# Attention and gated feed-forward on one core: the x of chunk 0 on GpSimd, earlier weight conversions, row sums turned with the last tile, the last rows in two halves

## The chip, the cores and the metric

The kernel runs on one core of a Trainium2 chip. A core has five engines that run side by side and wait for each other by semaphores: TensorE (PE, with its weight loads shown as PEld), VectorE (DVE), ScalarE (ACT), GpSimd (POOL), and SyncE (SP), which here only issues DMAs. The time is that of one execution on the device, in microseconds (us); the median of several runs counts. A span is the time from the first to the last instruction in a profile.

## What is computed

The reference, cut to what matters (4 batches, 8 heads, 576 positions, head dimension 64; then 2304 tokens, 512 columns, 1536 hidden columns):

```python
scores = scale * np.matmul(q, k.transpose(0, 1, 3, 2)) + bias      # bias: an MLP of relative positions, per head
attn = np.exp(scores - np.max(scores, axis=-1, keepdims=True))
attn = attn / (np.sum(attn, axis=-1, keepdims=True) + 1e-09)
x = np.matmul(attn, v)  # -> [2304, 512]
gate = 1.0 / (1.0 + np.exp(-(x @ w_gate)))
out = (gate * (x @ w_val)) @ w_out
```

All products are done to nearly fp32: an operand is split into a high part in a reduced format (`hi`, `aH`, `xhi`, `gh`) and the rest (`lo`, `aL`, `xlo`, `gl`), and hi·hi, hi·lo and lo·hi are summed.

## The kernel before

**Three stages.** First the bias of all heads is made and kept. Then attention runs over 16 units; unit u is a pair of heads p = u // 4 and a batch b = u % 4. Then the feed-forward part (class `Moe`) runs over 6 chunks of 384 tokens and 12 blocks f of 128 hidden columns.

**A unit of attention** has 9 steps s; n = 9u + s counts them all. A step issues, in an order that is written by hand: `score(n)` on TensorE into `sc`; `soft`, on DVE an operation that scales, adds the bias and takes the minimum (`en`, `mn`; L553), then on ACT the exponential with the row sum (L556); `turn(n - 2)`, which transposes an earlier `en` on TensorE into `pt` (L572, L592, and at step 8 L577), after which ACT writes `aH` and DVE writes `aL` (`split`, L471 and L472). For the steps in `AR` it is ACT that copies `pt` to `ar` and GpSimd that makes both parts (L465, L476). A few matmuls of `products` of the unit before fill each step (`FILL`); they sum in one PSUM buffer `acc`, so a new group of products can begin only when the copy `xe<-acc` (L635) on DVE has emptied it. `xe` goes to DRAM (`xs`).

**Row sums.** The nine columns of sums of a unit stand in the tile `sm`. `invert` adds 1e-9 on ACT (L611) and takes the reciprocal on DVE over 128 partitions and 9 columns (L612). `normal` transposes the result on TensorE (L598), DVE copies it to `rt` (9 partitions, 128 columns; L602), and two DMAs write it to `rs`.

**x of a chunk.** For each of the 4 head pairs kc, `load_x` and `load_r` fetch `xin` and `xrec` from `xs` and `rs`, and `prep_x` adds two halves (L797), multiplies by the reciprocal sums (L798), writes `xhi` on ACT (L799) and `xlo` (L800). For chunk 0 the table `PLAN` says at which step of the last four units (pair 3, steps counted from its first) each happens: l, r, x are loads and steps of chunk 0, capital letters those of chunk 1, s is one `stage`, the load of one more weight block. In chunk 0 only the add stands on GpSimd.

**Feed-forward.** For each (chunk, f) TensorE does 24 matmuls of `gates` into `pg` and `pu` (L864), then 9 of `outs` for the pair before (L885). In between, `gated` computes sigmoid on ACT, a product on DVE, and the split into `gh` and `gl` (L872 to L875). Chunks 0 (A) and 1 (B) are interleaved: A0 A1 B0 A2 B1 and so on. Weight blocks f = 0 and 1 are converted before; the others arrive as raw tiles `ww` and are made by `convert()`: on ACT L187, on DVE L190 to L199, on ACT `w<-wm` (L831), on DVE the lower part (L836). One call of `convert` begins one block and brings every begun block one stage on; a block is whole with its fifth call.

The instruction lists of all engines are in program order, and each engine runs its list in order.

Of the kernel before, what the change touches and what calls it, by code (L numbers as in the profile page):

```python
# [10 lines left out]
F32 = mybir.dt.float32  # L11
F32R = mybir.dt.float32r
# [3 lines left out]
AF = mybir.ActivationFunctionType  # L16
ALU = mybir.AluOpType

B, H, S, D = 4, 8, 576, 64
HID = 32  # L20
NT, DM, DFF = 2304, 512, 1536
NP = H // 2
# [3 lines left out]
FILL = (7, 0, 9, 0, 6, 3, 2, 7, 2)  # L26
ENB = 7
WM = 4
# [9 lines left out]
DPOS = [20, 36, 52], [6, 22, 38]  # L38
WARM = 12
CFI = 1  # L40
# [5 lines left out]
CONV = (2, 1)  # L46
START = 'X0 R1 X0 R2 X1 X2 X1 L3 s X2 X1 X1', 'R3 s X2 s s X3 X3 X2 X3 s X3'
XNEXT = {5: (("l", 0), ("r", 0)), 6: (("l", 1),), 7: (("p", 0), ("r", 1), ("l", 2)), 8: (("p", 1), ("r", 2), ("l", 3)),
# [3 lines left out]
PLAN = {  # L52
# [3 lines left out]
RAWS, WTS = 11, 18  # L56
SLOTS = (15, 18)
XENG = lambda nc, c: nc.vector if c else nc.gpsimd
AR = (1, 4, 7)
SOFT = (2, 7, 5, 3)  # L60
# [356 lines left out]
def attention(tc, att, q, k, v, biases, biasL, ident, xs, rs, extra):  # L417
# [3 lines left out]
    nc = tc.nc  # L421
# [3 lines left out]
    per = pool("per", 1)  # L425
# [4 lines left out]

    tiny = per.tile([128, 1], F32, name="tiny")
    nc.gpsimd.memset(tiny, 1e-9)
    QS = []
# [74 lines left out]
    vp = pool("vp", 1)  # L508
    enp = pool("enp", ENB)
    st = pool("st", 4)  # L510
    rtp = pool("rtp", 2)
    atp = pool("atp", 3)
    at4 = pool("at4", 2)
    ar_p = pool("arp", 2)
    xep = pool("xep", 2)
# [12 lines left out]
    def score(n):  # L528
        u, s = divmod(n, 9)
        p, b = units[u]  # L530
        ks, qs = prepped[u]
        if s == 0:
            state[u] = (st.tile([128, 9], F32, name="sm"), [], [], at4.tile([128, 2, S], F32R, name="a4"), {})
        ps = ps_s.tile([128, 2, 512], F32, name="sc")
        en = enp.tile([128, S], F32, name="en")
        sm = state[u][0][:, s:s + 1]
        state[u][4][s] = en
        if s < 8:
            h, it = divmod(s, 4)
# [12 lines left out]
        def soft():
            nc.vector.tensor_tensor_reduce(  # L553
                out=half(en), in0=ps[:, :, 0:HF], in1=half(nbias), scale=-0.125, scalar=3.0e38,
                op0=ALU.add, op1=ALU.min, accum_out=mn)
            nc.scalar.activation(out=en, in_=en, func=AF.Exp, bias=mn, scale=-1.0, accum_out=sm)  # L556

        return soft

    def turn(n):  # L560
# [12 lines left out]
        if s == 8:  # L573
            for h in range(2):
                after.append(split(aH[h][:, :, 512:576], aL[h][:, :, 512:576], pt[:, :, 64 * h:64 * h + 64]))
            pt = ps_t.tile([128, 4, 128], F32, name="pt")
            nc.tensor.transpose(pt[0:64, 0], en[:, 512:576], ident)  # L577
            last = normal(u, pt)
            after.append(split(a4[0:64, :, 512:576], a4[64:128, :, 512:576], pt[0:64, 0].rearrange("p (h i) -> p h i", h=2)))
            return after + [last]  # L580
        h, it = divmod(s, 4)
        i = slice(128 * it, 128 * it + 128)
        if s in AR:
            ar = ar_p.tile([128, 4, 128], F32, name="ar")
            nc.scalar.activation(out=ar, in_=pt, func=AF.Copy)
            pool_split(aH[h][:, :, i], aL[h][:, :, i], ar)
        else:
            after.append(split(aH[h][:, :, i], aL[h][:, :, i], pt))
# [6 lines left out]

    def normal(u, pt):
        p, b = units[u]
        nc.tensor.transpose(pt[0:9, 2], state[u][0], ident)  # L598
        rt = rtp.tile([9, 128], F32, name="rt")

        def leave():
            nc.vector.tensor_copy(out=rt, in_=pt[0:9, 2])  # L602
            to = rs[2 * p:2 * p + 2, S * b:S * b + S]
            nc.sync.dma_start(out=to[:, 0:512].rearrange("h (i p) -> h i p", p=128), in_=rt[0:8])
            nc.sync.dma_start(out=to[:, 512:576].rearrange("(o h) p -> o h p", o=1), in_=rt[8:9].rearrange("o (h p) -> o h p", h=2))

        return leave

    def invert(u):
        sm = state[u][0]  # L610
        nc.scalar.activation(out=sm, in_=sm, func=AF.Identity, bias=tiny)  # L611
        return lambda: nc.vector.reciprocal(out=sm, in_=sm)  # L612

# [29 lines left out]
    with tc.manual_schedule():  # L643
        work = iter(())
        after, due, loads, slow = [], [], [], []
        for n in range(9 * NU + LAG + 1):
            u, s = divmod(n, 9)
            soft = score(n) if n < 9 * NU else None
            inverse = invert(u - 1) if s == 0 and u > 0 else None
            later = turn(n - LAG) if LAG <= n < 9 * NU + LAG else []  # L650
# [21 lines left out]
            after = later  # L672
            if inverse:
                inverse()
            if s == WSTEP and 0 < u < NU:
# [22 lines left out]
class Moe:  # L698
# [53 lines left out]
    def do(self, what, eng=None):  # L752


        for w in what.split():
            i, c = int(w[1:] or 0), w[0] in "LRX"
            if w == "s":
                self.stage(eng)
            elif w == "t":
# [33 lines left out]
    def prep_x(self, c, t, r, hi, lo, kc):  # L793
        nc = self.nc
        x = t[:, 0]

        return [lambda: XENG(nc, c).tensor_tensor(out=x, in0=x, in1=t[:, 1], op=ALU.add),  # L797
                lambda: nc.vector.tensor_tensor(out=x, in0=x, in1=r, op=ALU.mult),  # L798
                lambda: nc.scalar.activation(out=hi[:, kc], in_=x, func=AF.Copy),  # L799
                lambda: nc.vector.tensor_tensor(out=lo[:, kc], in0=x, in1=hi[:, kc].bitcast(F32), op=ALU.subtract)]  # L800

# [85 lines left out]
    def store(self, c):  # L887
        for t, po in enumerate(self.po.pop(c)):
            if c == self.NC - 1 and t == 2:
                ob = self.pools["xin"].tile([128, 2, self.T], F32, name="xin").rearrange("p s t -> p (s t)")[:, 0:DM]  # L890
            else:
                ob = self.pools["ob"].tile([128, DM], F32, name="ob")
            self.nc.scalar.activation(out=ob, in_=po, func=AF.Copy)
            self.nc.sync.dma_start(out=self.out[self.T * c + 128 * t:self.T * c + 128 * t + 128, :], in_=ob)

    def run(self):
# [5 lines left out]
        with ExitStack() as ph, tc.manual_schedule():  # L902
# [6 lines left out]
            for i, cf in enumerate(order + [None]):  # L909
# [15 lines left out]
                for _ in range(CONV[c] - 1 if c < 2 else 0):  # L925
                    if self.going:
                        self.convert()
# [3 lines left out]
                if stored is not None:  # L931
                    self.store(stored)
                if self.going:
                    self.convert()
# [40 lines left out]
```

## Time and profile before

| | |
|---|---|
| median of 3 runs | 831.36 us (830.24 to 833.17) |
| profiled execution, its own time | 831.11 us |
| its span | 829.2 us |
| mean granted TensorE clock | 0.989 |
| TensorE matmuls busy | 797.5 us, 96% of the span |
| DVE, ACT, POOL busy | 61%, 52%, 31% |
| attention, about | 107 to 372 us |
| feed-forward, about | 362 to 826 us (its first gates stand among the last products of attention) |

In the page's slices TensorE is at nine tenths or more nearly throughout; the granted clock is full but for two places, near 317 to 323 us and near 388 to 395 us. The 1.9 us between span and time lie outside the instructions.

### The profile page before, as it was taken

What the parts mean: (1) busy time and instruction counts of PE and PEld (TensorE: products, weight loads), DVE (VectorE), ACT (ScalarE), POOL (GpSimd) and SP (SyncE); (2) the same over time, 40 slices, a digit from 0 to 9 for tenths busy, and PEclk for the clock granted to TensorE, in tenths of its full rate; (3) what the DMA queues carried; (4) which work ended last, traced back from release to release, by engine and by line L of the source; (5) the groups of instructions that cost most, each with busy time, mean ns of one, the idle gap of its engine ahead of it and who ended that gap; (6) DMA issues with size and microseconds to landing.
All of it is one profiled execution on the core that took longest, in us unless ns stands there. A gap on an engine that the chain in (4) does not pass through costs nothing.

```text
span 829.2 us, 16938 instructions
## 1 busy us (share of the span) xinstructions
PE 797.5 (96%) x6500; PEld 748.4 (90%) x6500; DVE 506.3 (61%) x1093; ACT 433.4 (52%) x918; POOL 261.2 (31%) x312
## 2 busy tenths in 40 slices
PE   7999989999999998977999999999999999999998
PEld 4888879999999998977999998999999999999997
DVE  6788879999998899966887884312411321241111
ACT  6888779899898996844444443211221221122112
POOL 1333669999998997730000000000000000000000
PEclk9999999999999998998999999999999999999999
DMA  5444336656556488749513301210030103011001
GB/s 192 130 146 146 97 75 171 164 134 185 148 158 170 140 241 230 216 155 355 192 52 104 99 1 52 89 51 28 10 115 1 40 30 85 0 39 39 1 1 38
DMA packets 51135, 89.56 MB, mean 108 GB/s; under 512 B 5616, under 2 KB 27248, under 8 KB 51056
## 3 DMA queue, kind: packets, MB, share of 16 engines
q1 hardware_dynamic: 48512, 85.28, 35.1%
q10 hardware_dynamic: 2544, 3.21, 1.2%
q8 instruction: 51, 0.84, 0.4%
q14 instruction: 28, 0.23, 0.1%
HBM read 61.66 MB, written 17.38 MB: 95 GB/s over the span
## 4 chain that ended last, share of the span: by engine, by line
PE 80%; DVE 12%; ACT 4%; issue 3%; DMA 0%; DVEq 0%; ACTq 0%
PE pg L864 18%; PE pu L864 18%; PE po L885 17%; PE acc L629 8%; PE sc L549 8%; PE pt L572 6%; PE bps L342 2%; DVE btmp L350 2%; ACT ind L323 1%; PE pt L592 1%; DVE bias L358 1%; DVE en L553 1%; PE y L318 1%; DVE xin L798 1%; ACT en L556 1%
## 5 line engine op out<-in xcount | busy, mean ns | idle before, releaser
L864 PE MATMUL pg<-xhi,w 128*128 128x384 f32 x576 | 161.1, 340 | 7.8 <-ACT w L831 2.8
L873 DVE TENSOR_TENSOR g<-pu,g 128x384 f32<-128x384 f32 x72 | 40.0, 556 | 209.6 <-PE pu L864 205.3
L864 PE MATMUL pu<-xhi,w 128*128 128x384 f32 x576 | 159.0, 336 | 0.0
L885 PE MATMUL po<-w,gh 128*128 128x512 f32 x432 | 133.8, 391 | 0.0
L556 ACT ACTIVATE en<-en,mn 128x576 f32<-128x576 f32 x144 | 111.5, 775 | 29.7 <-DVE mn L553 28.4
L864 PEld LDWEIGHTS pg<-xhi,w 128*128 128x128 f32 x576 | 105.9, 190 | 12.4 <-DVE w L836 3.3
L874 ACT ACTIVATE gh<-g 128x384 fp32r<-128x384 f32 x72 | 37.8, 525 | 147.9 <-DVE g L873 147.9
L549 PE MATMUL sc<-k,QS 128*128 128x288 f32 x640 | 112.8, 303 | 1.3 <-DVE bias L358 0.6
L864 PEld LDWEIGHTS pu<-xhi,w 128*128 128x128 f32 x576 | 105.2, 188 | 0.4 <-DVE w L836 0.4
L553 DVE CUSTOM_DVE_ANT_0 en<-sc,bias 128x576 f32<-128x576 f32 x128 | 94.0, 752 | 7.5 <-PE sc L549 6.5
L864 PE MATMUL pg<-xlo,w 128*128 128x384 f32 x288 | 97.5, 338 | 0.2 <-DVE xlo L800 0.2
L864 PE MATMUL pu<-xlo,w 128*128 128x384 f32 x288 | 96.7, 336 | 0.0
L549 PEld LDWEIGHTS sc<-k,QS 128*128 128x128 f32 x640 | 93.0, 191 | 2.4 <-PE sc L549 0.8
L872 ACT ACTIVATE g<-pg 128x384 f32<-128x384 f32 x72 | 35.1, 488 | 110.0 <-PE pg L864 108.9
L572 PE MATMUL pt<-ident,en 128*128 128x128 f32 x576 | 87.5, 275 | 3.6 <-DVE aL L472 2.6
L885 PEld LDWEIGHTS po<-w,gh 128*128 128x128 f32 x432 | 80.1, 188 | 12.0
L885 PE MATMUL po<-w,gl 128*128 128x512 f32 x216 | 84.2, 390 | 0.0
L629 PE MATMUL acc<-aH,vv 128*128 128x288 f32 x256 | 81.1, 334 | 3.0 <-DVE xe L635 1.9
L572 PEld LDWEIGHTS pt<-ident,en 128*128 128x128 f32 x576 | 69.1, 141 | 6.8 <-ACT en L556 3.1
L629 PE MATMUL acc<-aL,vv 128*128 128x288 f32 x256 | 71.6, 297 | 0.0
L472 DVE TENSOR_TENSOR aL<-pt,aH 128x512 fp32r<-128x512 f32 (+1 forms) x112 | 66.6, 607 | 7.1 <-ACT aH L471 7.1
L342 PE MATMUL bps<-cfs,ind 128*128 128x64 bf16 x1458 | 67.4, 193 | 3.2 <-DVE bias L358 2.5
(115 smaller groups left out, 1415.8 us busy)
## 6 DMA issues: line engine op xcount, KB each, us to landing
kr<-in_k_dram SPq DMA_DIRECT2D x32, 288.0 KB, 4.9
QS<-part SPq DMA_DIRECT2D x64, 144.0 KB, 2.6
xs<-xe SPq DMA_DIRECT2D x32, 288.0 KB, 3.9
xin<-xs SPq DMA_DIRECT2D x48, 192.0 KB, 3.5
vr<-in_v_dram SPq DMA_DIRECT2D x16, 320.0 KB, 3.7
qr<-in_q_dram SPq DMA_DIRECT2D x16, 288.0 KB, 3.6
xrec<-rs SPq DMA_DIRECT2D x48, 96.0 KB, 3.3
ww<-in_moe_w_out_dram SPq DMA_DIRECT2D x9, 512.0 KB, 6.9
```

The lines of the kernel that those rows point to most:

```text
L342: nc.tensor.matmul(out=o, lhsT=st, rhs=cfs[:, part], start=(part == 0), stop=(part == 2))
L472: return lambda: nc.vector.tensor_tensor(out=lo, in0=ps, in1=hi.bitcast(F32), op=ALU.subtract)
L549: nc.tensor.matmul(out=ps[:, e, 0:HF], lhsT=l, rhs=r[:, HF * e:HF * e + HF], start=(i == 0), stop=(i == len(mms) - 1))
L553: nc.vector.tensor_tensor_reduce(out=half(en), in0=ps[:, :, 0:HF], in1=half(nbias), scale=-0.125, scalar=3.0e38, op0=ALU.add, op1=ALU.min, ...
L556: nc.scalar.activation(out=en, in_=en, func=AF.Exp, bias=mn, scale=-1.0, accum_out=sm)
L572: nc.tensor.transpose(pt[:, J], en[:, 128 * J:128 * J + 128], ident)
L629: nc.tensor.matmul(out=acc[:, 0:HF], lhsT=l, rhs=r, start=(i == 0), stop=(i == len(mms) - 1))
L864: self.nc.tensor.matmul(out=(pg, pu)[z], lhsT=l, rhs=r, start=(kc == 0 and i == 0), stop=(kc == 3 and i == 2))
L872: nc.scalar.activation(out=g, in_=pg, func=AF.Sigmoid)
L873: nc.vector.tensor_tensor(out=g, in0=pu, in1=g, op=ALU.mult)
L874: nc.scalar.activation(out=gh, in_=g, func=AF.Copy)
L885: self.nc.tensor.matmul(out=po, lhsT=l[:, tt], rhs=r, start=(f == 0 and i == 0), stop=(f == self.NF - 1 and i == 2))
```

## The change

Nine things change together. (1) 16 instead of 12 warm-up matmuls. (2) The last tile of a unit (step 8) gets ten more columns, and the sums are written there (`en8`); the transpose of step 8 takes 73 columns instead of 64 and turns the sums with it. The transpose of `sm`, `invert` and `tiny` go. `normal` adds 1e-9 on DVE and takes the reciprocal there, over 9 partitions and 128 columns. (3) The tiles `en` get 6 buffers instead of 7, `ar` one instead of two. (4) In the last four units step 4 is split by ACT and DVE and no longer by GpSimd (`AR_LAST`). (5) The multiply and the subtract of x of chunk 0 move from DVE to GpSimd. (6) `PLAN` is rewritten. (7) Five loads of weight blocks, which stood among the steps of `START` and were issued by ACT, now stand first in it and are issued by SP. (8) `convert()` is also called when raw tiles wait though nothing has been begun, so it begins after the first gates and not at A2. (9) The last 128 rows leave as two halves: ACT copies and sends the left, DVE copies the right and SP sends it.

```diff
-ENB = 7
+ENB = 6
-WARM = 12
+WARM = 16
-START = 'X0 R1 X0 R2 X1 X2 X1 L3 s X2 X1 X1', 'R3 s X2 s s X3 X3 X2 X3 s X3'
+START = 's s s s s X0 R1 X0 R2 X1 X2 X1 L3 X2 X1 X1', 'R3 X2 X3 X3 X2 X3 X3'
 PLAN = {
-    2: "l0 l1", 3: "r0", 4: "s", 5: "r1", 6: "s", 8: "l2", 9: "x1", 10: "x0", 12: "x1 r2", 13: "x1 x0", 14: "x1 x0",
+    2: "l0 r0", 3: "l1 r1", 5: "s", 6: "x0 x0", 7: "x0 x0", 10: "l2 r2", 12: "s", 14: "x1 x1", 15: "x1", 16: "x1 s", 17: "L1",
...
-AR = (1, 4, 7)
+AR, AR_LAST = (1, 4, 7), (1, 7)
...
+    en8 = pool("en8", 2)
-    ar_p = pool("arp", 2)
+    ar_p = pool("arp", 1)
...
-            state[u] = (st.tile([128, 9], F32, name="sm"), [], [], at4.tile([128, 2, S], F32R, name="a4"), {})
+            last = en8.tile([128, S + 10], F32, name="en8")
+            state[u] = (last, [], [], at4.tile([128, 2, S], F32R, name="a4"), {8: last[:, 0:S]})
...
-            nc.tensor.transpose(pt[0:64, 0], en[:, 512:576], ident)
+            nc.tensor.transpose(pt[0:73, 0], sm[:, 512:S + 9], ident)
...
-        if s in AR:
+        if s in (AR if p < NP - 1 else AR_LAST):
...
-        nc.tensor.transpose(pt[0:9, 2], state[u][0], ident)
-            nc.vector.tensor_copy(out=rt, in_=pt[0:9, 2])
+            nc.vector.tensor_scalar(out=rt, in0=pt[64:73, 0], scalar1=1e-9, scalar2=None, op0=ALU.add)
+            nc.vector.reciprocal(out=rt, in_=rt)
...
-    def invert(u):
-        sm = state[u][0]
-        nc.scalar.activation(out=sm, in_=sm, func=AF.Identity, bias=tiny)
-        return lambda: nc.vector.reciprocal(out=sm, in_=sm)
...
-                self.stage(eng)
+                self.stage()
...
+        e = XENG(nc, c)
-        return [lambda: XENG(nc, c).tensor_tensor(out=x, in0=x, in1=t[:, 1], op=ALU.add),
-                lambda: nc.vector.tensor_tensor(out=x, in0=x, in1=r, op=ALU.mult),
+        return [lambda: e.tensor_tensor(out=x, in0=x, in1=t[:, 1], op=ALU.add),
+                lambda: e.tensor_tensor(out=x, in0=x, in1=r, op=ALU.mult),
                 lambda: nc.scalar.activation(out=hi[:, kc], in_=x, func=AF.Copy),
-                lambda: nc.vector.tensor_tensor(out=lo[:, kc], in0=x, in1=hi[:, kc].bitcast(F32), op=ALU.subtract)]
+                lambda: e.tensor_tensor(out=lo[:, kc], in0=x, in1=hi[:, kc].bitcast(F32), op=ALU.subtract)]
...
+            if c == self.NC - 1 and t == self.T // 128 - 1:
+                l, r = slice(0, DM // 2), slice(DM // 2, DM)
+                self.nc.scalar.activation(out=ob[:, l], in_=po[:, l], func=AF.Copy)
+                self.nc.scalar.dma_start(out=rows[:, l], in_=ob[:, l])
+                self.nc.vector.tensor_copy(out=ob[:, r], in_=po[:, r])
+                self.nc.sync.dma_start(out=rows[:, r], in_=ob[:, r])
...
-                    if self.going:
+                    if self.going or self.raw:
                         self.convert()
...
-                if self.going:
+                if self.going or self.raw:
                     self.convert()
```

The next lists are pieces of an engine's instructions in program order. First DVE in any unit from the second on, at its steps 1 to 3, before (`aL` and `a` are the lower parts of the last tile of the unit before, `bias_72` is the bias, the shape is that of the output):

```order
L472 TENSOR_TENSOR aL<-pt,aH 128x4x64 x2
L472 TENSOR_TENSOR a_4032<-pt,a_4032 64x2x64
L602 COPY rt<-pt 9x128
L553 ISA en,mn<-sc,bias_72 128x576
L553 ISA mn 128x1
L635 COPY xe<-acc 128x288
```

And the same place in the change, whose line numbers differ by a few (L554 is L553 of before, L632 is L635):

```order
L470 TENSOR_TENSOR aL<-pt,aH 128x4x64 x2
L470 TENSOR_TENSOR a_4027<-pt,a_4027 64x2x64
L603 TENSOR_SCALAR rt<-pt 9x128
L604 RECIPROCAL rt<-rt 9x128
L554 ISA en,mn<-sc,bias_72 128x576
L554 ISA mn 128x1
L632 COPY xe<-acc 128x288
```

A reciprocal of 128 columns now stands ahead of the softmax of step 3 and of the copy that empties `acc`.

Second, GpSimd in the first unit of the last pair, from its step 6 on, before (`k`, `vv` and `part` prepare k, v and q of the next unit):

```order
L465 TENSOR_SCALAR aH<-ar 128x4x128
L476 TENSOR_TENSOR aL<-ar,aH 128x4x128
L465 TENSOR_SCALAR vv_6379<-vr 128x5x64
L476 TENSOR_TENSOR vv_6379<-vr,vv_6379 128x5x64
L465 TENSOR_SCALAR k<-kr 128x576
L476 TENSOR_TENSOR k<-kr,k 128x576
L465 TENSOR_SCALAR aH<-ar 128x4x128
L476 TENSOR_TENSOR aL<-ar,aH 128x4x128
L797 TENSOR_TENSOR xin<-xin 128x384
```

And in the change:

```order
L792 TENSOR_TENSOR xin<-xin 128x384
L793 TENSOR_TENSOR xin<-xin,xrec 128x384
L463 TENSOR_SCALAR vv_6346<-vr 128x5x64
L474 TENSOR_TENSOR vv_6346<-vr,vv_6346 128x5x64
L795 TENSOR_TENSOR xlo<-xin,xhi 128x384
L463 TENSOR_SCALAR k<-kr 128x576
L474 TENSOR_TENSOR k<-kr,k 128x576
L463 TENSOR_SCALAR aH<-ar 128x4x128
L474 TENSOR_TENSOR aL<-ar,aH 128x4x128
```

The two operations on `ar` of step 4 have gone, and the add, the multiply and the subtract of x have come, around the preparation of v.

Third, ACT where attention ends and the feed-forward part begins, before (`xe` are the last products of attention, `g` the sigmoid of A0, `ww` raw weight blocks):

```order
L633 ACTIVATE xe<-acc 128x288 x3
L872 ACTIVATE g<-pg 128x384
L874 ACTIVATE gh<-g 128x384
L814 DMA ww<-in_moe_w_val_dram 128x4x256
L799 ACTIVATE xhi<-xin 128x384
```

And in the change:

```order
L630 ACTIVATE xe<-acc 128x288 x4
L794 ACTIVATE xhi<-xin 128x384
L187 ACTIVATE wm<-ww 128x512
L867 ACTIVATE g<-pg 128x384
L869 ACTIVATE gh<-g 128x384
L794 ACTIVATE xhi<-xin 128x384 x2
L187 ACTIVATE wm<-ww 128x512 x2
```

An `xhi` of chunk 1 and the first operation of the first conversion now stand ahead of the sigmoid of A0, and the DMA issues have left the engine.

## Rows read from the trace of the kernel before

**Rows 1.** The page: busy time, share of the span, instructions of each engine.

```profile
PE 797.5 (96%) x6500; PEld 748.4 (90%) x6500; DVE 506.3 (61%) x1093; ACT 433.4 (52%) x918; POOL 261.2 (31%) x312
```

**Rows 2.** Stretches: length; busy PE, PEld, DVE, ACT, POOL; granted clock, DMA share, GB/s.

```profile
200.00:250.00 50.00, 50.00 (x404) 49.72 (x403) 45.88 (x116) 45.67 (x111) 45.70 (x51) 1.00 0.61 167
...
300.00:340.00 40.00, 36.57 (x265) 35.35 (x264) 36.27 (x81) 31.30 (x75) 33.72 (x36) 0.91 0.87 237
340.00:360.00 20.00, 18.90 (x148) 17.83 (x147) 18.77 (x43) 16.81 (x41) 12.56 (x15) 1.00 0.55 169
...
372.00:400.00 28.00, 22.79 (x108) 20.75 (x108) 18.93 (x36) 12.43 (x23) 0.00 (x0) 0.88 1.02 342
```

**Rows 3.** Timeline of DVE in one unit: start, duration (us), line, operation.

```profile
182.61 0.21 DVE L612 RECIPROCAL sm<-sm 128x9 f32<-128x9 f32 x1
...
186.75 0.28 DVE L602 COPY rt<-pt 9x128 f32<-9x128 f32 x1
186.96 0.75 DVE L553 CUSTOM_DVE_ANT_0 en<-sc,bias 128x576 f32<-128x576 f32 x1
...
187.63 0.45 DVE L635 COPY xe<-acc 128x288 f32<-128x288 f32 x1
...
197.80 0.21 DVE L612 RECIPROCAL sm<-sm 128x9 f32<-128x9 f32 x1
```

**Rows 4.** Timeline of PE in the same unit.

```profile
187.71 0.60 PE L572 MATMUL pt<-ident,en 128*128 128x128 f32 x4
188.14 0.40 PE L629 MATMUL acc<-aH,vv 128*128 128x288 f32 x1
```

**Rows 5.** Groups by line: busy us, mean ns of one, idle before.

```profile
L602 DVE COPY rt<-pt 9x128 f32<-9x128 f32 x16 | 4.5, 279 | 0.5
...
L598 PE MATMUL pt<-ident,sm 128*9 128x128 f32 x16 | 4.4, 273 | 0.0
...
L612 DVE RECIPROCAL sm<-sm 128x9 f32<-128x9 f32 x16 | 3.4, 215 | 1.3 <-ACT sm L611 0.6
...
L263 DVE RECIPROCAL et<-et 128x1 f32<-128x1 f32 x1 | 0.2, 164 | 0.0
```

**Rows 6.** Timeline of DVE in the second unit of the last pair.

```profile
310.25 1.68 DVE L798 TENSOR_TENSOR xin<-xin,xrec 128x384 f32<-128x384 f32 x1
...
312.53 1.66 DVE L798 TENSOR_TENSOR xin<-xin,xrec 128x384 f32<-128x384 f32 x1
```

**Rows 7.** Timeline of PE in the last pair: idle before, and its releaser, in brackets.

```profile
315.61 0.63 PE L572 MATMUL pt<-ident,en 128*128 128x128 f32 x4 [2.16 <-DVE aL L472]
316.88 0.58 PE L629 MATMUL acc<-aH,vv 128*128 128x288 f32 x1 [0.64 <-DVE xe L635]
...
356.22 0.40 PE L629 MATMUL acc<-aH,vv 128*128 128x288 f32 x1 [0.66 <-DVE xe L635]
```

**Rows 8.** Timeline of POOL in the second unit of the last pair.

```profile
306.76 1.01 POOL L797 TENSOR_TENSOR xin<-xin 128x384 f32<-128x384 f32 x1
```

**Rows 9.** Timeline of DVE where the feed-forward part begins.

```profile
368.69 0.56 DVE L798 TENSOR_TENSOR xin<-xin,xrec 128x384 f32<-128x384 f32 x1 [3.83 <-DMA xrec<-rs]
...
390.32 0.68 DVE L836 TENSOR_TENSOR w<-wm,w 128x512 fp32r<-128x512 f32 x1
...
393.04 0.68 DVE L836 TENSOR_TENSOR w<-wm,w 128x512 fp32r<-128x512 f32 x1
```

**Rows 10.** Timeline of ACT in the same stretch.

```profile
372.42 0.48 ACT L872 ACTIVATE g<-pg 128x384 f32<-128x384 f32 x1
...
384.78 1.78 ACT L187 ACTIVATE wm<-ww 128x512 f32<-128x512 f32 x3
```

**Rows 11.** The chain that ended last, there: start, duration, engine, line.

```profile
372.95 2.37 PE pg L864 x12
...
394.62 2.16 PE pu L864 x12
```

**Rows 12.** Timeline of the last instructions.

```profile
825.62 0.60 ACT L893 ACTIVATE xin<-po 128x512 f32<-128x512 f32 x1
```

More of the change, by code (lines that the diff above doesn't have):

```diff
@@ L52 @@
 PLAN = {
[3 rows of a table removed]
+    2: "l0 r0", 3: "l1 r1", 5: "s", 6: "x0 x0", 7: "x0 x0", 10: "l2 r2", 12: "s", 14: "x1 x1", 15: "x1", 16: "x1 s", 17: "L1",
+    20: "l3 r3", 21: "s", 23: "x2 x2", 24: "x2", 25: "x2 s", 26: "L0", 27: "R0", 29: "s", 32: "x3 x3", 33: "x3", 34: "x3 L2",
+    35: "X0", 37: "t X0"}
 RAWS, WTS = 11, 18
@@ L428, in attention @@
     yield
-    tiny = per.tile([128, 1], F32, name="tiny")
-    nc.gpsimd.memset(tiny, 1e-9)
     QS = []
@@ L532, in score @@
         if s == 0:
-            state[u] = (st.tile([128, 9], F32, name="sm"), [], [], at4.tile([128, 2, S], F32R, name="a4"), {})
+            last = en8.tile([128, S + 10], F32, name="en8")
+            state[u] = (last, [], [], at4.tile([128, 2, S], F32R, name="a4"), {8: last[:, 0:S]})
         ps = ps_s.tile([128, 2, 512], F32, name="sc")
-        en = enp.tile([128, S], F32, name="en")
-        sm = state[u][0][:, s:s + 1]
-        state[u][4][s] = en
+        if s < 8:
+            state[u][4][s] = enp.tile([128, S], F32, name="en")
+        en = state[u][4][s]
+        sm = state[u][0][:, S + s:S + s + 1]
         if s < 8:
@@ L648, in attention @@
             soft = score(n) if n < 9 * NU else None
-            inverse = invert(u - 1) if s == 0 and u > 0 else None
             later = turn(n - LAG) if LAG <= n < 9 * NU + LAG else []
@@ L672, in attention @@
             after = later
-            if inverse:
-                inverse()
             if s == WSTEP and 0 < u < NU:
@@ L892, in store @@
                 ob = self.pools["ob"].tile([128, DM], F32, name="ob")
-            self.nc.scalar.activation(out=ob, in_=po, func=AF.Copy)
-            self.nc.sync.dma_start(out=self.out[self.T * c + 128 * t:self.T * c + 128 * t + 128, :], in_=ob)
+            rows = self.out[self.T * c + 128 * t:self.T * c + 128 * t + 128, :]
+            if c == self.NC - 1 and t == self.T // 128 - 1:
[4 more added lines that the diff above has]
+                self.nc.sync.dma_start(out=rows[:, r], in_=ob[:, r])
+            else:
+                self.nc.scalar.activation(out=ob, in_=po, func=AF.Copy)
+                self.nc.sync.dma_start(out=rows, in_=ob)
     def run(self):
```

2 rows, old and new, of the table PLAN are left out of this document.

## The prediction

> **What bounds the kernel now.** I read the page first: TensorE is busy for 96% of the span [rows 1], so only work taken from it, or waits and slow clock on it, can pay. Then the stretches: in the middle of attention TensorE is busy for 50.00 of 50.00 us, but DVE, ACT and GpSimd for about 45.8 each [rows 2]. TensorE sets the pace there, and three engines follow it closely. Two stretches stand out. From 300 to 360 us TensorE is idle for 3.43 + 1.10 us and its granted clock falls to 0.91 in the mean of the first 40 us; from 372 to 400 us it is idle for 5.21 us at a mean of 0.88 [rows 2]. [...] A stretch with a mean of 0.91 over 40 us holds about 2 x 0.09 x 40 = 7 us at the lower level and has lost half of that, 3.6 us; by the same reckoning the second has lost 0.12 x 28 = 3.4 us.
>
> The waits of TensorE name the causes. In the last pair it waits for `aL` and `xe` on DVE, 2.16 and 0.64 us one after the other [rows 7], just behind two multiplies of x on DVE that took 1.68 and 1.66 us [rows 6]; the same operation takes 0.56 us later, when GpSimd has nothing to do [rows 9]. At A2 it waits for weights: the first conversion begins at 384.78 [rows 10], while the first gates of the feed-forward part stand long before.
>
> **Row sums, the units of attention.** Removed for each unit: a transpose on TensorE, an ACT operation and a small reciprocal, 0.215 us [rows 5]. Transposes follow each other at (0.60 - 0.27)/3 = 0.11 us, from four of them [rows 4] and the length of one [rows 5], so TensorE gains 0.11 us for each unit. What ACT and the small reciprocal cost lies beside TensorE.
>
> Added: a reciprocal over 128 columns on DVE. No row shows one of that size. The nearest have 1 column, 0.164 us, and 9 columns, 0.215 us [rows 5]: 0.0064 us for each further column, and so 0.164 + 127 x 0.0064 = 0.97 us. The other bound is an operation without a price for a column beyond the ordinary, as the copy of the same shape, 0.28 us [rows 5]. I take 0.97, since two rows of the same operation outweigh one of another.
>
> What is queued behind it is what matters. In the list of DVE it stands ahead of the softmax of step 3 and the copy `xe`, which empties the only `acc`. Before, this copy began at 187.63 and ended at 188.08, and TensorE began its next product at 188.14, right after four transposes from 187.71 on, which end their turn 0.44 us later, at 188.15 [rows 3, 4]. So there is no slack: the copy ends just when TensorE needs `acc`. The copy of `rt` held the place of 0.21 us there, from 186.75 to 186.96 [rows 3]; now an add takes 0.28 and the reciprocal, which needs its result, about 0.9 until the next operation can begin. That is 1.2 instead of 0.2, 1.0 more. DVE comes to the place up to 0.15 us earlier, because ACT has an operation less ahead of the split that it waits for, while TensorE is there 0.11 us earlier. TensorE then waits for about 1.0 - 0.15 + 0.11 = 0.95, and a unit lasts 0.95 - 0.11 = 0.8 longer. The unit of now lasts 15.19 us, from one small reciprocal to the next [rows 3]. Twelve units have this place in the paced stretch (the second to the thirteenth): 12 x 0.8 = **+9.6 us**. With the short reciprocal the same sum gives 0.3 - 0.04 - 0.11, about 0.15 for each unit, +1.8.
>
> [...]
>
> **x of chunk 0, the last pair.** The multiplies and subtracts leave DVE, and with them the idle time and the slow clock of 300 to 360 us can go: 3.43 + 1.10 + 3.6 = 8.1. Three units there (the fourteenth to the sixteenth) pay for the reciprocal too: 3 x 0.8 = 2.4. DVE takes the `aL` of step 4 in exchange, some 0.6 us, which falls into time in which it waits for ACT. GpSimd does the three operations of x at about 1 us each, as its add took 1.01 [rows 8], and loses the copy and subtract of step 4 in each unit, about as much, so its load stays. But `xhi` now stands on ACT between two exponentials and waits for GpSimd, which has k to prepare first, with DMAs that are crowded there (0.87 of their time [rows 2]). I put 0.8 for that; from nothing to a wait like that of 2.16 [rows 7] in each of two units. The part: -8.1 + 2.4 + 0.8 = **-4.9**, between -8 and -1.
>
> **Early conversions.** Five calls of `convert` now come before A2, so block (2, 0) is whole and (2, 1) needs one more. Of the loss from 372 to 400, 0.95 us lies before A1 [rows 11]; the rest is 4.3 of waiting and 3.4 of clock, 7.7. What comes in its place: ACT has an `xhi` and a first conversion step (about 0.5 and 0.6, from 1.78 for three [rows 10]) ahead of the sigmoid of A0, which began at 372.42 [rows 10] and released A1 at 372.95 [rows 11]: 1.2 later. And on DVE the lower half of (2, 0) stands behind the product and split of B0, that of (2, 1) another 2.7 later (one block follows another at 393.04 - 390.32 [rows 9]), while TensorE reaches the second block of A2 some 2.1 after the first (2.16 for twelve matmuls [rows 11]): between 1 and 3 us of waits in all, 2.1 taken. 7.7 - 1.2 - 2.1 gives **-4.4**. If these pauses again bring the lower clock, it is nearer to -1; without them -6.5. The five loads that SP now issues first stand ahead of the `xrec` of chunk 1, for which DVE had already waited 3.83 us [rows 9]; up to A1 the products of attention cover that, behind it they would cost what they are late.
>
> **The ends.** The last copy of 0.60 us [rows 12] becomes two of half the size side by side: -0.3, between nothing and -0.6. Four more warm-up matmuls fill a pause of TensorE before its first real work, when DVE is what the others wait for: -0.2, between nothing and -0.5. Fewer buffers for `en` and `ar`: a buffer of `ar` is asked for again three steps later, some 5 us, and GpSimd is done with it after 2.5; an `en` is free once its last transpose has passed, which TensorE does in order before the scores that need it again. I cost both at nothing; what hides it is that GpSimd follows closely, and if it fell behind by 2 us, ACT would wait.
>
> **The sum.** +9.6 - 4.9 - 4.4 - 0.3 - 0.2 = -0.2, against the profiled execution's own 831.1 us: 830.9. The median shown is 0.25 above that execution, so I predict **831 us**: gains at two places, paid back in small change by each unit.
>
> **The rivals.**
> - *The reciprocal is short.* If it costs what the copy costs, the units lose 1.8 instead of 9.6 and the last pair 0.5 instead of 2.4: 831 - 7.8 - 1.9, about 821. For it speaks that two rows of 1 and 9 columns say little about 128; against it, that sixteen reciprocals of 9 columns agree on 0.215.
> - *GpSimd holds ACT (slower).* It is slower than before if GpSimd comes to `xhi` late by more than 2 us in three of the four units: the exponentials behind it are late, TensorE waits for them, and the clock falls once more as it did after 2.16 and 0.64. Then the last pair keeps its 8.1 and the 2.4 come on top: about 836. DMAs are busy at 0.87 there; but the loads of x now have four steps of time, and GpSimd's load is no higher.
> - *The conversions come no earlier in effect.* If the weights are waited for by ACT ahead of a sigmoid, or `xrec` is late, the second gain goes: 835. Against it: the first raw blocks are asked for several us earlier than before.
> - *The reciprocal is longer still.* Two rows with few columns fix a slope badly: a quarter more, 1.2 us, adds 0.24 to each of fifteen units, 3.6, and gives about 834.5. Against it, the rows' slope is 6.4 ns. [...]
>
> **How the numbers follow.** Forecast with the reciprocal at about 0.9 to 1.0 us: 0.43, its own range 828 to 834. Short reciprocal, or one that is partly hidden: 0.27, 820 to 828. GpSimd holds ACT: 0.13, 834 to 838. Conversions without effect: 0.10, 833 to 836. Longer reciprocal: 0.07, 833 to 836. A measurement of this kernel can tell 0.3%, 2.5 us, from no change. Faster by more than that has the second case and some 0.15 of the forecast, 0.42; slower has most of the last three, 0.25; 0.33 remains. The range that leaves out 2 in 10 goes from 820.5 to 836.
>
> **What would show it.** A RECIPROCAL `rt` of 0.9 to 1.0 us in the groups by line, and `PE acc <- DVE xe` with about 0.9 us some fifteen times among the waits; the distance from one copy of `rt` to the next near 16.0 instead of 15.19. From 300 to 360 us full clock and no wait for `aL`. The first `wm<-ww` near 373 instead of 384.78, and A2 done some 4 us earlier after the end of attention. The prediction is wrong first of all if the reciprocal lasts 0.3 us, or if TensorE's products do not wait for that copy.

## The result, and the profile after

The changed kernel takes 839.51 us (837.44 to 841.41, 4 runs) against 831.18 us: 1.010 times the time before, 95% interval 1.0082 to 1.0118. Measured a second time (changed_again, below) it takes 837.22 us, ratio 1.0063 [1.0044, 1.0083]. Both times it is slower. The execution profiled first has 837.44 us of its own and a span of 835.6: 6.3 and 6.4 us more than the profiled execution of before. The medians differ by 2.0 us more than that; why the four runs of the first time lie 2 us above the six of the second stays open.

**A unit of attention.** The list of waits of TensorE (what waited for what: us in total, times, the longest):

```profile
PE acc L626 <- DVE xe L632: 15.2, 15, 1.0
...
PE pg L859 <- ACT g L867: 2.6, 1, 2.6
...
PE sc L550 <- DMA QS<-part: 1.3, 1, 1.3
```

Before, the wait for `xe` was seen only in the last pair [rows 7]. Now it stands in 15 units. DVE's timeline, then TensorE's, at the place of [rows 3, 4], then lines of the next unit, of A1 (near 380 us) and of the tail (831.90):

```profile
190.54 0.28 DVE L470 TENSOR_TENSOR a<-pt,a 64x128 fp32r<-64x128 f32 x1
190.85 0.28 DVE L603 TENSOR_SCALAR rt<-pt 9x128 f32<-9x128 f32 x1
191.17 0.94 DVE L604 RECIPROCAL rt<-rt 9x128 f32<-9x128 f32 x1
192.15 0.76 DVE L554 CUSTOM_DVE_ANT_0 en<-sc,bias 128x576 f32<-128x576 f32 x1
...
192.83 0.45 DVE L632 COPY xe<-acc 128x288 f32<-128x288 f32 x1
...
207.43 0.94 DVE L604 RECIPROCAL rt<-rt 9x128 f32<-9x128 f32 x1
...
380.99 0.56 DVE L793 TENSOR_TENSOR xin<-xin,xrec 128x384 f32<-128x384 f32 x1 [7.31 <-DMA xrec<-rs]
...
831.90 0.42 DVE L893 COPY xin<-po 128x256 f32<-128x256 f32 x1 [2.73 <-ACT xin L891]
```

```profile
191.72 0.60 PE L573 MATMUL pt<-ident,en 128*128 128x128 f32 x4
193.34 0.41 PE L626 MATMUL acc<-aH,vv 128*128 128x288 f32 x1 [1.02 <-DVE xe L632]
...
383.09 0.44 PE L859 MATMUL pg<-xhi,w 128*128 128x384 f32 x1 [2.57 <-ACT g L867]
```

The reciprocal lasts 0.94 us and the wait behind it 1.02. From one reciprocal to the next it is 207.43 - 191.17 = 16.26 us, where a unit lasted 15.19.

**The stretches** (columns as in [rows 2]):

```profile
200.00:300.00 100.00, 93.87 (x748) 92.45 (x748) 89.94 (x209) 84.47 (x198) 85.36 (x94) 1.00 0.53 145
300.00:340.00 40.00, 36.94 (x294) 36.17 (x293) 37.19 (x87) 34.43 (x83) 36.65 (x40) 1.00 0.83 232
340.00:371.00 31.00, 27.04 (x211) 25.97 (x210) 27.25 (x61) 24.27 (x58) 21.71 (x25) 1.00 0.62 196
371.00:403.00 32.00, 27.77 (x144) 25.62 (x145) 19.56 (x39) 12.71 (x25) 0.42 (x2) 0.95 1.02 331
...
383.09:388.95 5.86, 5.86 (x25) 5.86 (x26) 2.95 (x7) 1.66 (x4) 0.00 (x0) 0.71 0.99 310
```

TensorE, busy throughout the middle of attention before, is idle for 6% of it; its granted clock is full up to 371 us, so the slow clock of the last pair has gone. One stretch at a low clock remains, behind the wait of 2.57 us at A1: from the start of A1 to `po`, the last row, the mean is 0.71 (0.50 from 385 to 387 us).

**Where 6.4 us of span come from**, by marks that both traces have:

| | before | after | difference |
|---|---|---|---|
| first `rt` (L602, L603) | 126.05 | 125.81 | -0.24 |
| from there over 12 units | 182.35 | 195.16 | +12.81 |
| last pair, three units | 54.31 | 50.16 | -4.15 |
| A0 starts | 362.51 | 370.93 | +8.42 |
| from there to the end of A2 | 34.12 | 31.59 | -2.53 |
| from there to the end of the span | 432.6 | 433.1 | +0.5 |

### The profile page after: what moved, and what is told of

Same layout as the page of the kernel before. It is cut to its first block, busy times and chain, and to the rows that moved or that the text cites. A ratio compares the mean times of both kernels' runs of the same rounds, so it can differ in the third digit from the quotient of the medians.

```text
span 835.6 us, 16810 instructions
## 1 busy us (share of the span) xinstructions
PE 793.8 (95%) x6488; PEld 743.6 (89%) x6488; DVE 512.8 (61%) x1090; ACT 431.3 (52%) x902; POOL 260.2 (31%) x311
## 4 chain that ended last, share of the span: by engine, by line
PE 71%; DVE 13%; ACT 9%; issue 3%; DMA 3%; SPq 1%; POOL 0%; ACTq 0%; DVEq 0%; POOLq 0%
PE pu L859 17%; PE po L880 16%; PE pg L859 16%; PE acc L626 6%; PE sc L550 6%; PE pt L573 4%; ACT en L557 2%; PE bps L342 2%; DVE en L554 2%; DVE btmp L350 2%; ACT aH L469 2%; PE pt L593 1%; DVE bias L358 1%; ACT ind L323 1%; DMA xrec<-rs 1%
## 5 line engine op out<-in xcount | busy, mean ns | idle before, releaser
L550 PE MATMUL sc<-k,QS 128*128 128x288 f32 x640 | 111.0, 299 | 2.6 <-DMA QS<-part 1.3
L554 DVE CUSTOM_DVE_ANT_0 en<-sc,bias 128x576 f32<-128x576 f32 x128 | 94.1, 754 | 8.9 <-PE sc L550 7.4
L626 PE MATMUL acc<-aH,vv 128*128 128x288 f32 x256 | 80.4, 331 | 16.4 <-DVE xe L632 15.2
L470 DVE TENSOR_TENSOR aL<-pt,aH 128x512 fp32r<-128x512 f32 (+1 forms) x116 | 69.5, 611 | 7.8 <-ACT aH L469 7.8
```

The costliest lines, as they stand in the source:

```text
L470: return lambda: nc.vector.tensor_tensor(out=lo, in0=ps, in1=hi.bitcast(F32), op=ALU.subtract)
L554: nc.vector.tensor_tensor_reduce(out=half(en), in0=ps[:, :, 0:HF], in1=half(nbias), scale=-0.125, scalar=3.0e38, op0=ALU.add, op1=ALU.min, ...
L626: nc.tensor.matmul(out=acc[:, 0:HF], lhsT=l, rhs=r, start=(i == 0), stop=(i == len(mms) - 1))
```

## The experiments

All ratios are against the kernel before, run on the same chip. A unit is the distance of two `rt` in the paced stretch; A0 and A2 are the start of A0 and the time from there to the end of A2's gates (in rt_on_act one more group of products stands ahead of A0, so its marks are left out).

| run | median | ratio [95%] | unit | A0 | A2 |
|---|---|---|---|---|---|
| before | 831.2 to 832.7 | 1 | 15.19 | 362.51 | 34.12 |
| sums_only | 843.56 | 1.0149 [1.0125, 1.0172] | 16.27 | 374.86 | 33.36 |
| x0_only | 826.5 | 0.9939 [0.9918, 0.996] | 15.17 | 356.77 | 35.23 |
| early_conv_only | 831.68 | 1.0002 [0.9989, 1.0015] | 15.17 | 361.47 | 34.67 |
| changed_again | 837.22 | 1.0063 [1.0044, 1.0083] | 16.26 | 370.32 | 31.57 |
| sums_narrow | 828.85 | 0.997 [0.9955, 0.9986] | 15.28 | 358.38 | 37.85 |
| recip_later | 827.93 | 0.9957 [0.9941, 0.9972] | 15.52 | 358.87 | 34.37 |
| xrec_first | 836.32 | 1.006 [1.0042, 1.0077] | 16.26 | 370.89 | 30.40 |
| narrow_xrec_first | 826.62 | 0.9938 [0.9917, 0.9958] | 15.28 | 358.40 | 34.72 |
| conv_act_queue | 828.98 | 0.9959 [0.9941, 0.9977] | 15.19 | 363.33 | 32.37 |
| x_before_most | 821.64 | 0.9877 [0.9855, 0.9898] | 15.17 | 357.84 | 28.22 |
| x_before_all | 821.46 | 0.9877 [0.9858, 0.9896] | 15.17 | 358.12 | 28.18 |
| same_partitions | 822.26 | 0.9882 [0.9864, 0.9901] | 15.30 | 359.81 | 27.76 |
| rt_on_act | 824.29 | 0.9905 [0.9886, 0.9924] | 15.29 | | |
| buffers_tail, rt_to_64 | 832.66, 830.7 (one run each) | | 15.19, 15.18 | | |

**One part at a time.** sums_only, x0_only and early_conv_only are the kernel before with one part of the diff each: (2) with (3), (4) to (6), and (7) with (8).

> The kernel before with only the edit of the row sums (merged transpose, add and reciprocal over 128 columns, buffers of en and ar as in the changed kernel). Theory (the parts add up): twelve units at 1.07 us more and three in the last pair that pay between nothing and 1.07 each, 831.2 + 12.9 to 16.1 = 844 to 847 us. Rival (a part of the longer unit comes from x of chunk 0 or from loads at other places): a unit of 16.0 us or less, 841 us or less.

> The kernel before with only x of chunk 0 on GpSimd, the changed PLAN and AR_LAST. In the changed kernel the last pair took 50.1 us for three units of at least 16.27, here the units are 15.2 apart: theory, the last pair takes 47 to 48 us instead of 54.3, attention ends 6 to 7 us earlier, and the feed-forward part starts with more waiting for weights, 825 to 828 us. Rival (GpSimd holds ACT at xhi): the pair takes 51 us or more, 829 us or more.

> The kernel before with only the early conversions (START, weight loads on SP, convert called while raw blocks stand). Theory (the loads ahead of xrec delay A1, the conversions relieve A2): DVE waits 7 us or more for xrec, A1 starts 1.5 to 7 us later after A0 than the 10.4 of before, A2 has no wait left; together -3 to +2 us, 829 to 833 us. Rival (as predicted, only ACT's two operations ahead of the sigmoid count): A1 1.2 us later, 827 us.

By the ratios +12.4 us, -5.1 and +0.2, 7.5 together, about what the whole change costs (5.2 to 8.3). Part by part the sum is less exact: from A0 to A2 the early conversions alone cost 0.5 us and in the changed kernel go with a gain of 2.5. The row sums are the loss, a little below the 844 to 847 us of their theory, since the last pair pays nothing for them (53.4 us for three units, 54.3 before). x of chunk 0 gives about what its theory said: three units in 48.4 us instead of 54.3. The early conversions give nothing: A2's waits are gone but for 0.37 us, but DVE's timeline shows a wait in their place, and TensorE waits 5.69 us for `g` at A1:

```profile
374.62 1.03 DVE L798 TENSOR_TENSOR xin<-xin,xrec 128x384 f32<-128x384 f32 x2 [11.27 <-DMA xrec<-rs]
```

```profile
376.73 0.69 PE L864 MATMUL pg<-xhi,w 128*128 128x384 f32 x1 [5.69 <-ACT g L872]
```

**The reciprocal: its length or its place?** Two versions of the changed kernel.

```diff
 sums_narrow:                                  # before the transpose, 9 columns
...
-            nc.vector.tensor_scalar(out=rt, in0=pt[64:73, 0], scalar1=1e-9, scalar2=None, op0=ALU.add)
-            nc.vector.reciprocal(out=rt, in_=rt)
+            nc.vector.tensor_copy(out=rt, in_=pt[64:73, 0])
...
+        sm = state[u][0][:, S:S + 9]          # invert(u), called where it was before
+        nc.scalar.activation(out=sm, in_=sm, func=AF.Identity, bias=tiny)
+        return lambda: nc.vector.reciprocal(out=sm, in_=sm)
 recip_later:                                  # 128 columns, behind the softmax of step 4
...
+            if held and s in (4, 5):
+                held.pop()()                  # reciprocal and the two DMAs
```

> The changed kernel, with the sums inverted before their transpose again (9 columns, as in the kernel before), and a copy of 9x128 behind it; the merged transpose and all else stay. Theory (the wide reciprocal ahead of the copy of acc is what lengthens a unit): TensorE's wait for xe goes, a unit lasts 15.1 us (15.19 less the saved 0.11) instead of 16.27, fifteen units give back 15 x 1.17 = 17.5 us, about 822 us. Rival (fewer buffers of en and ar, or ACT and GpSimd close behind TensorE, hold the units): other waits take its place, a unit stays at 15.6 us or more, 830 us or more.

> The changed kernel with the same reciprocal over 128 columns, moved behind the copy of acc and the softmax of step 4; only the add of 1e-9 stays at the old place. Theory (its place in DVE's list costs, not its length): the wait of 1.02 us for xe goes, a unit lasts 15.1 to 15.4 us, 822 to 827 us. Rival (DVE has no 0.8 us to spare in a unit, wherever it stands): TensorE waits for another result of DVE instead, a unit stays at 15.8 us or more, 833 us or more.

DVE's timeline of recip_later:

```profile
188.88 0.45 DVE L635 COPY xe<-acc 128x288 f32<-128x288 f32 x1
...
190.52 0.94 DVE L607 RECIPROCAL rt<-rt 9x128 f32<-9x128 f32 x1
191.38 0.68 DVE L554 CUSTOM_DVE_ANT_0 en<-sc,bias 128x576 f32<-128x576 f32 x1
```

Moved behind the copy of `acc`, the same 0.94 us cost a unit 0.33 instead of 1.07: the place was most of the price. Inverted early, the sums cost 0.09 a unit, which may be in the 0.33 too; how the rest comes about is not shown (DVE waits only twice in such a unit, 0.45 us each). Both expected times were too low, since the feed-forward part took back much of what the units gave, and the units are longer than both theories had them (15.1, and 15.1 to 15.4). In sums_narrow attention ends 12.5 us earlier than in the changed kernel, and A1 then waits 7.89 us for `g`. Its timelines of TensorE, DVE and SP say why:

```profile
375.87 0.69 PE L868 MATMUL pg<-xhi,w 128*128 128x384 f32 x1 [7.89 <-ACT g L876]
```

```profile
187.23 0.28 DVE L605 COPY rt<-pt 9x128 f32<-9x128 f32 x1
187.55 0.76 DVE L556 CUSTOM_DVE_ANT_0 en<-sc,bias 128x576 f32<-128x576 f32 x1
...
373.77 1.03 DVE L802 TENSOR_TENSOR xin<-xin,xrec 128x384 f32<-128x384 f32 x2 [13.50 <-DMA xrec<-rs]
```

```profile
360.25 0.39 SPq L818 DMA_DIRECT2D ww<-in_moe_w_gate_dram  x1
...
362.26 0.55 SPq L818 DMA_DIRECT2D ww<-in_moe_w_val_dram  x1
362.86 3.87 SPq L793 DMA_DIRECT2D xrec<-rs  x4
```

Five weight loads are issued, 512 KB each, and then two `xrec`, each as two DMAs of 96 KB; DVE starts on the first 10.9 us after the first of these issues. In the kernel before, where no five loads stood ahead, that took 7.0 us (361.72 to 368.69 [rows 9]). ACT's list holds the sigmoid behind the `xhi` that needs `xrec`, TensorE stands still, and its clock is low for most of A1 (granted 0.58 in the mean of the 6.9 us from A1's start to `po`; 4.3 us at full clock before).

**The order of the loads.** In START, R1 and R2 load the `xrec` of head pairs 1 and 2 of chunk 1 (the first two in START; that of pair 0 is loaded in the last unit), L3 and R3 the last `xin` and `xrec`, s is one weight load.

```diff
-START = 's s s s s X0 R1 X0 R2 X1 X2 X1 L3 X2 X1 X1', 'R3 X2 X3 X3 X2 X3 X3'
+START = 'R1 R2 s s s s s X0 X0 X1 X2 X1 L3 X2 X1 X1', 'R3 X2 X3 X3 X2 X3 X3'        # (narrow_)xrec_first
+START = 'R1 R2 s s X0 X0 X1 X2 X1 X1 X1 L3 R3 X2 s s s', 'X2 X3 X3 X2 X3 X3'        # x_before_most
+START = 'R1 R2 X0 X0 X1 X2 X1 X1 X1 L3 R3 X2 s s s s s', 'X2 X3 X3 X2 X3 X3'        # x_before_all
```

xrec_first and narrow_xrec_first are the changed kernel and sums_narrow with the first of these; x_before_most and x_before_all are the kernel before with the parts of x0_only and early_conv_only, and this order.

> The changed kernel, with the loads of the first two xrec of chunk 1 put ahead of the five weight loads on SP. Theory (A1 waits for g because ACT stands behind an xhi whose xrec was queued behind five weight loads): DVE's wait for xrec of 7.31 us is at most 3, A1 starts 10 to 10.5 us after A0 instead of 12.2, at full clock; 3 us less than the changed kernel, about 834.5 us. Rival (the loads of weights are late then and A2 waits instead): A2 waits for w by what A1 gains, no change in time.

> The changed kernel with both: the sums inverted over 9 columns before the transpose, and the first two xrec of chunk 1 loaded ahead of the weights. With the sums alone A1 waited 7.89 us for g and then ran 2.6 us longer at the slow clock, DVE having waited 13.5 us for xrec. Theory (order of the loads): most of these 10.5 us go, some 2 to 3 come back as waits of A2 for weights, 820 to 823 us. Rival (the DMA engines need this long for what is asked of them there, in whatever order): 826 us or more, the wait only moves to A2.

> The kernel before with x of chunk 0 on GpSimd and with the early conversions, but the loads in another order: the first two xrec of chunk 1, two weight loads, the last xin and xrec of chunk 1, then the other three weight loads. Theory (what the early conversions lacked was x of chunk 1 ahead of the weights): A1 starts 10.5 us after A0 as before, B0 and A2 wait 1 us at most, 6 to 7 us less than with x of chunk 0 alone (826.5), 819 to 822 us. Rival (the DMA engines are full from 363 us on, so that either x or the weights come late): a wait of 3 us or more stays at B0 or A2 with the slow clock behind it, 824 us or more.

> The same with all five weight loads behind x of chunk 1. Theory: x comes without a wait, the conversions begin 2 to 3 us later than with two loads ahead, A2 waits 1 to 3 us, 821 to 824 us. Rival (the amount of DMA decides, not the order): the same time as with two loads ahead.

xrec_first takes 1.2 us less from A0 to the end of A2 than changed_again (30.40 and 31.57), A1 starting 10.0 us after A0; less than its theory, as a wait of 1.68 us stands at B0. In the changed kernel SP's list holds `xrec` back in a second way, which the same edit undoes:

```profile
371.88 0.43 SPq L809 DMA_DIRECT2D ww<-in_moe_w_gate_dram  x1
373.71 0.65 SPq L606 DMA_DIRECT2D rs<-rt  x1
...
375.51 1.79 SPq L784 DMA_DIRECT2D xrec<-rs  x3
```

The write of the last unit's `rt` stands between the fourth and the fifth weight load. It is issued when the last reciprocal has ended (372.75 + 0.93 on DVE), and `xrec` behind it, 4.6 us after A0 began; DVE starts on it 5.5 us later. What the queue and what this delay cost is not told apart.

So with only R1 and R2 ahead the wait moves, and more of it in sums_narrow: in narrow_xrec_first A1 starts 10.0 us after A0, and B0 waits for `g`, held by the x of head pair 3, whose `xin` and `xrec` came late. R2, issued at 357.61, was used after 4.7 us (timelines of TensorE, then of DVE):

```profile
378.87 0.69 PE L868 MATMUL pg<-xhi,w 128*128 128x384 f32 x1 [3.94 <-ACT g L876]
```

```profile
362.34 0.56 DVE L802 TENSOR_TENSOR xin<-xin,xrec 128x384 f32<-128x384 f32 x1 [1.58 <-DMA xrec<-rs]
```

So 826.62 us is the rival's time: the wait only moved, though to B0 and not to A2. Its reason, that the DMA engines need this long in whatever order, does not hold, as the next two runs show. With all of x ahead of most of the weights the waits go, and the 28.2 us from A0 to the end of A2 are 6 less than before. Of TensorE's waits from A1 to A2, the list of x_before_most for 300 to 425 us has only these left:

```profile
...
PE pg L865 <- ACT g L873: 0.9, 1, 0.9
PE pu L865 <- DVE w L837: 0.4, 1, 0.4
```

Its windows show full clock from A0 to A2:

```profile
358.00:392.00 34.00, 31.60 (x173) 29.09 (x173) 23.39 (x47) 15.60 (x31) 0.33 (x2) 1.00 0.99 333
```

Both are 1.2% faster than before, and equal: whether two weight loads go ahead of x or none does not matter, and the 1 to 3 us at A2 that x_before_all expected did not come. The DMA engines are about as full (0.99) as in the changed kernel (1.02), so their load alone is not what held A1. One more run left the five early loads where the change has them, but in ACT's queue:

> As early_conv_only, but the five early weight loads are issued by ACT, in its DMA queue, as in the kernel before; the loads of x stay on SP's. Theory (xrec is late because it stands behind 2.5 MB of weights in the same queue): from another queue the weights hold it little, DVE waits 5 us or less for xrec instead of 11.27, A1 starts at most 11.5 us after A0, A2 ends 29 to 31 us after A0 instead of 34.67, 826 to 829 us. Rival (the 16 DMA engines are full, whatever the queue): the wait for xrec stays at 8 us or more and the time at 830 us or more.

828.98 us, as its theory had it: the wait for R1 and R2 is gone, a smaller one for the last `xrec` stays (2.95 us), and TensorE waits 2.36 us at B0, so that A2 ends 32.37 us after A0 and not 29 to 31. The instruction order on SP moved with it, `xrec` being issued at 362.55 and most weights later, so queue and order are not told apart.

**What is left in a unit.** sums_narrow saves a transpose, and its unit is still 0.09 us longer than before. Three runs looked for the cause.

```diff
-        rt = rtp.tile([9, 128], F32, name="rt")
+        rt = rtp.tile([128, 128], F32, name="rt")[64:73]     # same_partitions; rt_to_64: this alone, in the kernel before
-            nc.vector.tensor_copy(out=rt, in_=pt[64:73, 0])
+            nc.scalar.activation(out=rt, in_=pt[64:73, 0], func=AF.Copy)     # rt_on_act, rt on partitions 0 to 8
```

> As x_before_most, with the merged transpose of narrow sums (inverted over 9 columns) and the copy of rt kept on the partitions 64 to 72 that it reads from, instead of moving to 0 to 8; warm-up and tail as before. With the sums inverted early a unit took 15.28 us, the copy 0.32 us to the next operation's start, where the copy before, 0.28 long too, took 0.21. Theory (an operation that moves between partitions is not overlapped with the next): 0.21 again, a unit of 15.1 to 15.17 us. Rival (ENB of 6 or the one ar buffer hold the unit): 15.28 again. Time: 0 to 2 us below x_before_most, or 1 above.

> The kernel before, with the copy of rt written to the partitions 64 to 72 of its tile instead of 0 to 8; nothing else differs. [...] Theory (held start): the softmax of step 3 begins 0.31 us after the copy instead of 0.21, the copy itself lasts 0.28 as before, and as the copy of acc behind it had no slack, a unit lasts 15.28 to 15.30 us instead of 15.19. Rival (the longer units of the merged transpose came from something else, the single transpose of 73 columns or ACT): 0.21 and 15.19.

> As same_partitions, but the copy of rt is done by ACT, to partitions 0 to 8; the reciprocal stays over 9 columns ahead of the transpose. Theory (a unit is as long as DVE's way from the sums to the copy of acc makes it): that way is 0.3 us shorter, TensorE's wait before acc goes and the 0.11 of the saved transpose shows, a unit of 15.08 us, some 2 us below same_partitions, 820 us. Rival (ACT, which stands in turn with DVE, is late by what it took over): a unit of 15.2 us or more, 822 us or more.

In sums_narrow the softmax begins 0.32 us after the copy of `rt` (187.23 and 187.55, above). DVE's timeline of same_partitions, then of rt_to_64:

```profile
187.88 0.29 DVE L605 COPY rt<-pt 9x128 f32<-9x128 f32 x1
188.19 0.76 DVE L556 CUSTOM_DVE_ANT_0 en<-sc,bias 128x576 f32<-128x576 f32 x1
```

```profile
186.46 0.28 DVE L472 TENSOR_TENSOR a<-pt,a 64x128 fp32r<-64x128 f32 x1
186.67 0.27 DVE L602 COPY rt<-pt 9x128 f32<-9x128 f32 x1
186.97 0.76 DVE L553 CUSTOM_DVE_ANT_0 en<-sc,bias 128x576 f32<-128x576 f32 x1
```

Before, the copy began 0.32 us after `a` and the softmax 0.21 after the copy [rows 3]. With the sums on partitions 64 to 72 of `pt` both gaps are 0.29 to 0.33 (sums_narrow and same_partitions, twelve units each), wherever the copy goes: the theory of same_partitions fell. With `rt` written to partitions 64 to 72 from a source at partition 0 the gaps change places, 0.21 and 0.30, and the unit stays at 15.18; the expected 15.28 did not allow for the gap that closes. In these runs the gaps go with the partitions of the copy's input and output; what makes a gap long or short is not shown, and that an output at partition 64 brings the 0.31 was the assumption of rt_to_64's theory. From `a` to the softmax it is 0.53 us before (186.43 to 186.96) and 0.64 in sums_narrow (186.91 to 187.55): with the merged transpose 0.11 us more stand ahead of `xe`. rt_on_act takes the copy out of DVE's list, and a unit is still 15.29, as its rival had it: the transposes into `pt` now begin when ACT has copied `rt` out of it (timelines of ACT, then of TensorE):

```profile
188.02 0.27 ACT L605 ACTIVATE rt<-pt 9x128 f32<-9x128 f32 x1
```

```profile
188.34 0.66 PE L575 MATMUL pt<-ident,en 128*128 128x128 f32 x4
```

One unit later the copy ends at 203.31 + 0.27 = 203.58 and the transposes begin at 203.63. The profiled span of rt_on_act is 1.2 us longer than that of same_partitions; this arises behind A2, where the two kernels do not differ, and why is not shown.

**Buffers and tail**, in one kernel since the places are far apart: 6 `en`, 1 `ar`, and a tile of its own for the right half of the last rows.

> The kernel before with only 6 buffers of en and 1 of ar, and with the last 128 rows leaving in two halves whose right half has a tile of its own. Theory: the unit stays at 15.19 us (buffers cost nothing), and the halves now run side by side: the right half starts within 0.1 us of the left, the end comes 0.2 to 0.4 us earlier after the last matmul than the 4.0 of before. Rivals: a unit of 15.28 us; the right half still waits for the left (through po, which both read).

The buffers cost nothing, 15.19. The tail did not follow: DVE's copy starts when ACT's has ended (826.52 + 0.39, then 826.93), as in the changed kernel, where it is 831.90. So the end comes no earlier: 4.5 us after the last matmul began, 4.0 before. The rival holds in so far as the right half still waits for ACT's copy with a tile of its own, which leaves `po`, which both read; whether the chip or the program's own semaphores ask for that is not shown (DVE's timeline of buffers_tail).

```profile
826.93 0.42 DVE L899 COPY xin<-po 128x256 f32<-128x256 f32 x1 [2.73 <-ACT xin L896]
```

The changed kernel a second time:

> The changed kernel once more, for a second profile. 837 to 841 us; the span's profile was 2 us below the median, so a second one shows which stretch differs: the wait ahead of A1 and the slow clock behind it (by theory), or the units of attention (rival).

Its profile has the same waits (15.2 for `xe`, 2.51 at A1) and a span of 835.0; it shows no stretch that explains the first median.

## Why the prediction was wrong

The mechanism put first, a reciprocal ahead of the copy of `acc`, was the right one; at A1 the wait was one that the forecast had named and put at nothing. The forecast's sum of -0.2 measures +6.4: **four terms of it were mis-sized, all to the hopeful side**.

- **Row sums, +9.6, measured +12.8.** The step that failed is the one behind "TensorE then waits for about 1.0 - 0.15 + 0.11 = 0.95, and a unit lasts 0.95 - 0.11 = 0.8 longer". The reciprocal was right (0.97 forecast, 0.94 measured), and so was the queue behind it. But a unit grew by 1.07, nearly as much as DVE's way from `rt` to the end of `xe`: from 186.75 to 188.08 before, from 190.85 to 193.28 after, 1.33 and 2.43 us. So the 1.0 was 1.1. The 0.15 by which DVE was to come earlier did not come: `rt` starts 0.87 us ahead of TensorE's transposes now and started 0.96 ahead before, the 0.09 less being about what TensorE gained. And 0.95 - 0.11 is 0.84, rounded there to 0.8, which is 0.5 us over twelve units. The 0.11 of the transpose cancels in that sum, and in the runs it was no gain either, since a unit was as long as DVE's way made it. About 0.1 of the longer way lies between the reciprocal and the softmax: the softmax began 0.98 us after the reciprocal, the one in recip_later 0.86; why is not shown. At 100% busy TensorE already stood 0.08 us for `xe` before (0.43 from `pt` to `acc` [rows 4], 0.35 elsewhere in the unit):

```profile
191.37 0.60 PE L572 MATMUL pt<-ident,en 128*128 128x128 f32 x4
191.72 0.38 PE L629 MATMUL acc<-aH,vv 128*128 128x288 f32 x1
```

- **Early conversions, -4.4, measured -2.5.** A1 came 1.7 later, not 1.2, and for another reason: not ACT's own two operations but `xrec`, late behind the weights and, in SP's list, behind the write of the last `rt`. The prediction named these loads and costed them at nothing, since "up to A1 the products of attention cover that". They did not: 7.31 us of waiting on DVE, and 1.6 us of slow clock in A1, the case that it had at -1. At A2 it went about as forecast: waits of 0.20 and 0.37 are left, and from `po` to `po` around A2 it takes 5.8 us less, where 7.7 - 2.1 = 5.6 was forecast.
- **The last pair, -4.9, measured -4.15.** Idle time for `aL` and the slow clock have gone, as said. The 3.6 and 3.4 us of slow clock in the forecast's sums are reckoned with a lower level of half the clock; the trace of before has a granted clock of 0.50 from 317 to 323 us and from 388 to 394, and of 1.00 from 323 and from 395 on. The reciprocals cost 3.2 and not 2.4; beside them one unit is 1.5 longer (17.81), where `sc` waits 1.30 for `QS`, a DMA; GpSimd held ACT once, by 0.9.
- **The ends, -0.3 and -0.2, measured +0.5 and -0.24.** The halves run one after the other, and the end comes 4.6 us after the last matmul began instead of 4.0. The -0.24 is near the forecast, but one pair of profiles does not show it: the first `rt` starts at 125.95 to 127.30 in the kernels with 12 warm-up matmuls and at 125.80 to 126.16 in those with 16.

3.2 + 1.9 + 0.75 + 0.8 are the 6.6 us between sum and span. Of the rivals, slow GpSimd and the longer reciprocal, which came nearest to the measured time, were not what happened; and by its own terms the first gives 831 + 4.9 + 2.4 = 838, not 836. A further column of the reciprocal took (0.941 - 0.164)/127 = 6.1 ns, where the two rows gave 6.4.

## What to carry to other kernels

Price an added operation by how much longer it makes the chain of instructions that closes the loop (here rt, softmax, copy of `acc`), and count no gain of another engine against it, even one that is busy 100%: moved behind the copy, the same reciprocal cost a third. When work is pulled earlier, look at what its loads push back: with five weight loads ahead of small ones the early conversions brought nothing, and with x ahead of most or all of the weights they brought 5 us on top of x on GpSimd, and the kernel is 1.2% faster than before. Experiments with one part each showed in three runs that one part of the change cost more than the others brought.

## What was not expected of the hardware

- The softmax starts 0.21 us after the copy of `rt` in the kernel before and 0.32 after it in sums_narrow, with a copy of 0.28 us both times. With the nine sums at partition 64 of `pt` a unit lasted 15.28 (sums_narrow) and 15.30 us (same_partitions) instead of 15.19.
- Behind five loads of 512 KB in one queue, two DMAs of 96 KB were in use 10.9 us after the first was issued (sums_narrow); ahead of them, 4.7 us after (narrow_xrec_first, 357.61 to 362.34).
- A merged transpose saves TensorE some 0.11 us by the forecast's estimate, and no unit became shorter by it in four kernels (15.28 to 15.30 us).
